# Most causal masks of two batches taken off the matrix engine, one batch's x transposed by DMA, and the order of work composed anew, in an attention and SwiGLU kernel

## The chip, the cores and the metric

The kernel runs on one core of a Trainium2 chip. The metric is the device time of a run in microseconds (us), which lies some 1.7 us above the span that the profile shows. Runs of this kernel vary: 0.9% among the first four of the kernel before, and more on the chip of the experiments. Each run has a state: here "slow" means over 1.5% above the fastest run of the same kernel. Ratios compare runs of the state "fast" alone. Each run also lists TensorE's mean granted clock, as a share of full speed.

## The reference

Attention with 16 beacon keys per head in front of 576 causal keys, then a SwiGLU block on the result. Shortened:

```python
B, H, S, Nb, D = 8, 8, 576, 16, 64
k_all = concat([beacon_k, k], axis=2); v_all = concat([beacon_v, v], axis=2)
scores = q @ k_all.T / sqrt(D)
scores = where(causal, -1e9, scores)       # beacons are visible to all
a = softmax(scores)
x = (a @ v_all) as [4608 tokens, 512]
out = (silu(x @ w_gate) * (x @ w_val)) @ w_out     # d_ff = 1536
```

## The kernel before

One core does it all in bf16 with fp32 accumulation. The order of work on every engine is fixed by a string, the *list*, of one letter per piece. The letters that matter here are `s` (a unit of scores with its exp), `P` (value products of one head), `X` (x of two heads transposed on TensorE), `g` and `G` (part of, or a full, gate and value unit), `F` (one output matmul), `l` (a load issued by GpSimd), `c`/`C` (a regrouping copy on VectorE/GpSimd), `t` (a DMA transpose of k or q). A unit of scores covers two heads and up to 496 columns; four of them (A to D) make a pair of heads.

A causal mask is needed only on the diagonal blocks. It is made in one of two ways. In batches 0 and 1 TensorE adds -30000 to the scores with a matmul before the exp; in batches 2 to 7 GpSimd zeroes the upper triangle of p with a select after it:

```python
PE_MASKS = (0, 1)
NPEX = 2                    # batches whose x is transposed on TensorE

def mask_on_pe(u, ps):
    for hh in range(2):
        for col, n, d in UNITS[u][3]:
            nc.tensor.matmul(ps[:, hh, col : col + n], lhsT=below[:],
                             rhs=ident[:, d : d + n], start=False, ...)

def exponent(b, m, u, ps):
    nc.scalar.activation(p[:, :, c0 : c0 + w], ps[:, :, 0:w], ACT.Exp, scale=0.125)
    for col, n, d in [] if b in PE_MASKS else diagonals:
        nc.gpsimd.affine_select(out=ap, in_=ap, ...)

def scores(burst):
    tiles = [big.tile([P, 2, 512], FP32, ...) for _ in burst]
    # ... the score matmuls of all units of the burst; exponent() at once,
    # or, for b in PE_MASKS, mask_on_pe() and exponent() after them all
# [cut]
        elif kind == "P":
            pv(b, m, n % 2, *small())
            if b >= NPEX and n % 8 == 7:
                x_transpose(b)          # five DMA transposes issued by SyncE
```

GpSimd also issues the loads that cast fp32 to bf16, which is all but the first three. In the list they begin with v of batch 0, then all eight gate and value weight loads, then k, q and v of batch 1:

```python
start = v_loads(0, 0, H)
for i in range(4):
    start += w_loads(i)
start += k_loads(1, 0, H) + q_loads(1, 0, H) + v_loads(1, 0, H)
```

A full gate and value unit is eight matmuls of 512 columns into a two-bank PSUM tile, a tanh on ScalarE and two passes of VectorE. Three such tiles (`big`) serve units of scores and gate units alike.

The softmax here doesn't subtract the row's maximum and nothing guards it: scores larger than these inputs give would overflow.

## Time and profile before

| | kernel before |
|---|---|
| time, median of the first 3 runs | 377.18 us (374.79 to 377.33) |
| profiled run, its span | 374.0 us, 372.3 us |
| TensorE busy | 364.0 us, 98% |
| matmuls | 2919 |
| mask matmuls on TensorE / selects on GpSimd | 80 / 120 |
| first full gate unit starts (timeline) | 28.81 us |

The prediction below shows the page's lines. A digit in the rows of slices is the busy share of one fortieth of the span in tenths. A wait is put down to what ended it. A timeline row gives start, length, engine, line, operation, shapes, count and, in brackets, the idle time before it and what ended that. The length uses a modelled end, so the cost of a matmul is better read from the difference of two starts.

### The profile page before, as it was taken

To read this page: it belongs to the slowest core of one execution; us is meant where nothing else is said; L and a number is where in the kernel's file an instruction comes from. 1 tells how busy PE (TensorE), PEld (TensorE's weight loads), DVE (VectorE), ACT (ScalarE), POOL (GpSimd) and SP (SyncE) were. 2 spreads that over 40 slices of the span, in tenths; PEclk is the share of its full clock that TensorE was granted. 3 is DMA by queue.
4 is the path that set the end of the run, shared out by engine and by line. 5 is a ranking of instruction groups with operands and counts; after the bars stand their busy time and mean duration, and the time that the engine had idled before them with its cause. 6 is when DMAs were issued, how large, how long until landed. Compare 5 with 4: busy or idle time off the path is not lost.

```text
span 372.3 us, 7423 instructions
## 1 busy us (share of the span) xinstructions
PE 364.0 (98%) x2919; PEld 184.2 (49%) x2919; DVE 230.9 (62%) x432; ACT 170.3 (46%) x243; POOL 154.4 (41%) x267
## 2 busy tenths in 40 slices
PE   8999999999999989999999999999999999999996
PEld 4654466554454544445455445544545444444443
DVE  5848845477646658555658476477565764666652
ACT  3943389833673644455562536723751311321210
POOL 8847789992893590453390602810320000000000
PEclk9999999999999999999999999999999999999999
DMA  9999999999999999794798792742100311001012
GB/s 168 178 203 160 180 158 162 148 185 95 124 205 145 72 117 172 90 101 78 129 149 91 123 148 72 78 51 60 58 28 30 63 58 56 0 30 57 30 40 102
DMA packets 158516, 39.04 MB, mean 105 GB/s; under 512 B 146576, under 2 KB 154000, under 8 KB 158480
## 3 DMA queue, kind: packets, MB, share of 16 engines
q0 software_dynamic: 112304, 18.83, 73.6%
q1 hardware_dynamic: 45968, 19.43, 24.4%
q8 instruction: 23, 0.38, 0.4%
q10 hardware_dynamic: 208, 0.29, 0.3%
q14 instruction: 13, 0.11, 0.1%
HBM read 38.27 MB, written 9.44 MB: 128 GB/s over the span
## 4 chain that ended last, share of the span: by engine, by line
PE 93%; DMA 3%; DVE 1%; POOL 1%; ACT 1%; issue 0%; POOLq 0%; ACTq 0%
PE gv_ps L355 49%; PE o_ps L394 24%; PE pv_ps L310 7%; PE s_ps L286 7%; DMA vb<-in_v_dram 2%; PE s_ps L255 2%; DMA first_k<-in_k_dram 1%; PE t_ps L234 1%; PE o_ps L414 1%; PE xt_ps L329 1%; PE t_ps L210 1%; POOL p L269 1%; ACT p L266 1%; POOL vb L138 0%; DVE kT L196 0%
## 5 line engine op out<-in xcount | busy, mean ns | idle before, releaser
L368 ACT ACTIVATE th<-gv_ps 128x512 f32<-128x512 f32 x108 | 64.4, 597 | 163.7 <-PE gv_ps L355 160.0
L370 DVE SCALAR_TENSOR_TENSOR u<-th,gv_ps 128x512 f32<-128x512 f32 x108 | 74.1, 686 | 76.5 <-ACT th L368 75.6
L355 PE MATMUL gv_ps<-xT,wg 128*128 128x512 bf16 x432 | 112.8, 379 | 1.5 <-DVE hT L373 1.3
L394 PE MATMUL o_ps<-wo,hT 128*128 128x512 bf16 x420 | 113.3, 380 | 0.0
L355 PE MATMUL gv_ps<-xT,wv 128*128 128x512 bf16 x432 | 112.8, 379 | 0.0
L266 ACT ACTIVATE p<-s_ps 128x992 bf16<-128x992 f32 (+2 forms) x128 | 101.9, 866 | 18.8 <-PE s_ps L286 14.6
L269 POOL TENSOR_SCALAR_AFFINE_SELECT p<-p 128x256 bf16<-128x256 bf16 (+2 forms) x120 | 44.3, 398 | 108.6 <-ACT p L266 108.4
L373 DVE SCALAR_TENSOR_TENSOR hT<-gv_ps,u 128x512 bf16<-128x512 f32 x108 | 74.6, 691 | 3.7
L355 PEld LDWEIGHTS <-wv 128*128 128x128 bf16 x432 | 42.2, 98 | 50.7
L355 PEld LDWEIGHTS <-wg 128*128 128x128 bf16 x432 | 41.3, 98 | 48.6 <-issue 2.2
L394 PEld LDWEIGHTS <-hT 128*128 128x128 bf16 x420 | 37.5, 98 | 41.9 <-issue 5.7
L310 PEld LDWEIGHTS <-p 128*128 128x128 bf16 x960 | 36.6, 97 | 11.2 <-DVE x L319 0.4
L310 PE MATMUL pv_ps<-vb,p 128*128 128x65 bf16 x960 | 39.6, 193 | 1.0 <-DMA vb<-in_v_dram 1.0
L138 POOL DMA_DIRECT2D vb<-in_v_dram x40 | 34.3, 870 | 0.7 <-PE pv_ps L310 0.3
L286 PE MATMUL s_ps<-qT,kT 64*128 64x80 bf16 (+4 forms) x384 | 33.7, 281 | 0.6 <-ACT p L266 0.3
L319 DVE TENSOR_TENSOR x<-pv_ps,rec 128x320 bf16<-128x320 f32 x64 | 31.4, 491 | 2.6 <-DVE rec L318 0.4
L138 POOL DMA_DIRECT2D kb<-in_k_dram x35 | 30.0, 858 | 6.7 <-DMA wv<-in_moe_w_val_dram 4.2
L403 DVE COPY o_sb<-o_ps 128x512 f32<-128x512 f32 x35 | 24.0, 685 | 13.9 <-PE o_ps L394 13.7
L138 POOL DMA_DIRECT2D qb<-in_q_dram x35 | 30.2, 864 | 5.3 <-PE t_ps L234 2.0
L318 DVE RECIPROCAL rec<-pv_ps 128x5 f32<-128x5 f32 x64 | 12.2, 190 | 31.1 <-PE pv_ps L310 31.0
L286 PEld LDWEIGHTS <-kT 64*128 64x128 bf16 x384 | 14.7, 94 | 19.6 <-issue 12.9
L255 PE MATMUL s_ps<-ident,below 128*128 128x128 bf16 (+1 forms) x80 | 7.9, 217 | 0.0
(52 smaller groups left out, 87.9 us busy)
## 6 DMA issues: line engine op xcount, KB each, us to landing
out_dram<-o_sb SPq DMA_DIRECT2D x35, 256.0 KB, 2.7
qb<-in_q_dram POOLq DMA_DIRECT2D x28, 128.0 KB, 5.7
vb<-in_v_dram POOLq DMA_DIRECT2D x24, 128.0 KB, 5.3
kb<-in_k_dram POOLq DMA_DIRECT2D x21, 128.0 KB, 7.0
wg<-in_moe_w_gate_dram POOLq DMA_DIRECT2D x4, 384.0 KB, 9.9
wv<-in_moe_w_val_dram POOLq DMA_DIRECT2D x4, 384.0 KB, 11.1
wo<-in_moe_w_out_dram POOLq DMA_DIRECT2D x2, 768.0 KB, 9.1
vb<-in_v_dram POOLq DMA_DIRECT2D x8, 112.0 KB, 5.1
```

Source lines behind the costliest of these rows:

```text
L138: return eng.dma_start(dst[p0 : p0 + n, c, h0:h1, 0:D], src[b, h0:h1, r : r + n, :].rearrange("h j d -> j h d"))
L266: nc.scalar.activation(p[:, :, c0 : c0 + w], ps[:, :, 0:w], ACT.Exp, scale=0.125)
L269: nc.gpsimd.affine_select(out=ap, in_=ap, compare_op=ALU.is_ge, fill=0.0, base=d, pattern=[[0, 2], [1, n]], channel_multiplier=-1,)
L286: nc.tensor.matmul(ps[:, hh, col : col + n], lhsT=kT[b % 2][r, m, P * t : P * t + P], rhs=qT[b % 2][r, m, q0 : q0 + n], start=b not in PE_ ...
L310: nc.tensor.matmul(o_ps[:, c, 0 : D + 1], lhsT=pt[(NPAIR * b + m) % NPT][:, hh, col : col + P], rhs=vb[b % 2][:, t, h, 0 : D + 1], start=( ...
L319: nc.vector.tensor_tensor(out=xs[b][:, :, D * h : D * h + D], in0=o_ps[:, :, 0:D], in1=rec[:].to_broadcast([P, NKT, D]), op=ALU.mult,)
L355: nc.tensor.matmul(gvs[f][:, TOK * half : TOK * half + TOK], lhsT=w[:, kk, P * f : P * f + P], rhs=xT[:, kk, r : r + TOK], start=(kk == 0) ...
L368: nc.scalar.activation(th[:], ps[:, 0:TOK], ACT.Tanh, scale=0.5)
L370: nc.vector.scalar_tensor_tensor(out=u[:], in0=th[:], scalar=1.0, in1=ps[:, 0:TOK], op0=ALU.add, op1=ALU.mult)
L373: nc.vector.scalar_tensor_tensor(out=hTs[j][:, f, :], in0=ps[:, TOK:1024], scalar=0.5, in1=u[:], op0=ALU.mult, op1=ALU.mult)
L394: nc.tensor.matmul(st["o"][:], lhsT=hTs[j][:, f, P * i : P * i + P], rhs=wo[:, f, :], start=(f == 0), stop=(f == NF - 1),)
L403: nc.vector.tensor_copy(o_sb[:], st["o"][:])
```

## The change

The intent is to unload TensorE, which is busy all the time: masks of the first two batches go mostly behind the exp, to VectorE (a multiply with a 0/1 triangle, new letter `d`) or GpSimd (the select, letter `e`); x of batch 1 goes to DMA transposes as in later batches; 36 masks of batches 2 to 7 go from GpSimd to VectorE; and the list is composed anew, with the weight loads as letters `w` in it.

```diff
-NPEX = 2
+NPEX = 1
-PE_MASKS = (0, 1)
+    upper = static.tile([P, P + NB], BF16, name="upper")
-    def exponent(b, m, u, ps):
+    def exponent(b, m, u, mask, ps):
-        for col, n, d in [] if b in PE_MASKS else diagonals:
+        for col, n, d in [] if mask == "s" else diagonals:
             ap = p[:, :, c0 + col : c0 + col + n]
+            if mask == "d":
+                nc.vector.tensor_tensor(
+                    out=ap, in0=ap, in1=upper[:, None, d : d + n].to_broadcast([P, 2, n]), op=ALU.mult
+                )
+                continue
             nc.gpsimd.affine_select(
@@ [cut: the same test in scores()] @@
-    start = v_loads(0, 0, H)
-    for i in range(4):
-        start += w_loads(i)
-    start += k_loads(1, 0, H) + q_loads(1, 0, H) + v_loads(1, 0, H)
+    weights = [load for i in range(4) for load in w_loads(i)]
+    start = v_loads(0, 0, H) + k_loads(1, 0, H) + q_loads(1, 0, H) + v_loads(1, 0, H)
@@ [cut: 17 early parts of gate units become 9; all 20 lines of the list; the first two:] @@
-        "llllllclqlllKcllKssclQlcccslsllKlsQssKQsllllsPlP",
-        "ssPlsPXslossXPsllPgPlXollgPglgXlggglgllgGGlGlGGl",
+        "lllllllclQkcKeeQcdscwCwKeslcQssQKsswPwPeePPewXee",
+        "XPllsPgPxgllPwggXlllgwlgwogggGGllGGGGoGlGulGFddF",
```

More of the change, by code (lines that the diff above doesn't have):

```diff
@@ L177, in load_wo @@
         )
-    spare = []
     def parts_of(eng):
@@ L200, in transpose_pair @@
         h = slice(2 * m, 2 * m + 2)
-        while spare:
-            spare.pop()
-            nc.tensor.transpose(t_ps[:, 0:P], below[:], ident[:])
         first = n - 64
@@ L281, in scores @@
         tiles = [big.tile([P, 2, 512], FP32, name="s_ps", tag="big") for _ in burst]
-        for (b, m, u), ps in zip(burst, tiles):
+        for (b, m, u, mask), ps in zip(burst, tiles):
             for t, col, q0, n in UNITS[u][2]:
@@ L289, in scores @@
                         rhs=qT[b % 2][r, m, q0 : q0 + n],
-                        start=b not in PE_MASKS or col == 0,
-                        stop=b not in PE_MASKS,
-                    )
-            if b not in PE_MASKS:
-                exponent(b, m, u, ps)
-        for (b, m, u), ps in zip(burst, tiles):
-            if b in PE_MASKS:
+                        start=mask != "s" or col == 0,
+                        stop=mask != "s",
+                    )
+            if mask != "s":
+                exponent(b, m, u, mask, ps)
+        for (b, m, u, mask), ps in zip(burst, tiles):
+            if mask == "s":
                 mask_on_pe(u, ps)
-                exponent(b, m, u, ps)
+                exponent(b, m, u, mask, ps)
     xs = {}
@@ L453 @@
     )
+    nc.gpsimd.memset(upper[:], 1.0)
+    nc.gpsimd.affine_select(
+        out=upper[:],
+        in_=upper[:],
+        compare_op=ALU.is_ge,
+        fill=0.0,
+        base=0,
+        pattern=[[1, P + NB]],
+        channel_multiplier=-1,
+    )
     idle = big.tile([P, 1024], FP32, name="idle_ps", tag="big")
@@ L485 @@
     done = dict.fromkeys("SPKQUXgGFltwoc", 0)
-    first = ([(0, 0, 2), (1, 0, 2), (0, 2, 3), (1, 2, 3), (2, 0, 2), (2, 2, 3), (0, 3, 4), (1, 3, 4), (2, 3, 4)],
-             [(0, 0, 1), (0, 1, 2), (1, 0, 1), (1, 1, 2), (0, 2, 3), (1, 2, 3), (0, 3, 4), (1, 3, 4)])
-    parts = [(j, *part) for j in range(2) for part in first[j]]
-    units = [(j, f) for j in range(NCH) for f in range((3, 2, 0)[min(j, 2)], NF)]
+    first = [[(0, 0, 2), (1, 0, 2), (0, 2, 3), (1, 2, 3), (2, 0, 2), (2, 2, 3), (0, 3, 4), (1, 3, 4), (2, 3, 4)]]
+    parts = [(j, *part) for j in range(len(first)) for part in first[j]]
+    units = [(j, f) for j in range(NCH) for f in range((3, 0)[min(j, 1)], NF)]
     def free(b, values=False):
@@ L520, in piece @@
     def piece(kind):
-        n = done[{"C": "c", "k": "K", "q": "Q", "u": "U", "x": "X", "Y": "K", "Z": "Q", "s": "S"}.get(kind[0], kind[0])]
+        n = done[{"C": "c", "k": "K", "q": "Q", "u": "U", "x": "X", "Y": "K", "Z": "Q", "s": "S", "d": "S", "e": "S"}.get(kind[0], kind[0])]
         eng = nc.scalar if kind in "kqx" else nc.gpsimd if kind == "C" else None if kind in "YZ" else nc.vector
-        if kind[0] == "s":
+        if kind[0] in "sde":
             burst = []
@@ L531, in piece @@
                     assert done["U"] > i // 4 - 4 if b < NPE else done["t"] >= 10 * (b - NPE + 1)
-                burst.append((b, m, ("ABDC" if b == 0 else "ABCD")[i % 4]))
+                burst.append((b, m, ("ABDC" if b == 0 else "ABCD")[i % 4], kind[i - n]))
             scores(burst)
@@ L554, in piece @@
             assert done["X"] >= 4 * j + k1
+            assert done["w"] >= 2 * (f // 3) + 2
             gv_mm(j, f, k0, k1)
@@ L560, in piece @@
             assert j < NHT or done["F"] >= (j - NHT + 1) * 4 * NF
-            assert done["g"] >= (9, 17)[j] if j < 2 else done["P"] >= 8 * min(j + 1, B)
+            assert done["g"] >= 9 if j < 1 else done["P"] >= 8 * min(j + 1, B)
+            assert done["w"] >= 2 * (f // 3) + 2
             gv_unit(j, f)
@@ L570, in piece @@
         elif kind == "w":
-            spare.extend(range(4))
+            weights[n]()
         elif kind in "cC":
@@ L581, in piece @@
             turns[n]()
-        done[{"C": "c", "k": "K", "q": "Q", "u": "U", "x": "X", "Y": "K", "Z": "Q", "s": "S"}.get(kind[0], kind[0])] += len(kind)
+        done[{"C": "c", "k": "K", "q": "Q", "u": "U", "x": "X", "Y": "K", "Z": "Q", "s": "S", "d": "S", "e": "S"}.get(kind[0], kind[0])] += len(kind)
     one_bank = [(outp, "outp")]
@@ L586 @@
     plan = [
-        "llllllclqlllKcllKssclQlcccslsllKlsQssKQsllllsPlP",
-        "ssPlsPXslossXPsllPgPlXollgPglgXlggglgllgGGlGlGGl",
-        "GlGUGGsFFlFFusUlslFFssFFlssFFlFFPulssFllPssFPlll",
-        "FsslFllPssFPUsFtxUssXllFtlFUttstPlFFssslFlFPUsFF",
-        "FPsssFFFlPFtlFssglgPsllltlsFFFXtFggXgllgPFgFgtGP",
-        "GltGPFllGlGlFGFGFsstFFPFFtllstssFltPttlFGPllGlGF",
-        "FssFllFFFFsslsPFFFFFPstlssFFtFFFltPslsFFFFlPFFtF",
-        "lGGlGlFGFGFFssFPFFlFFFlsssFPFGPllFtGFFssPFtltFll",
@@ L595 @@
-        "lFFlsstsltPFFGPGFGlFGFGGGFFFstsFtFFFFltFFFFlssll",
-        "GGtFGPGFslsFFlFlFPtssstFFFtPltFFFGFFGFGFFPFFFFFF",
-        "FsslsPFFFFFlFPFstssFlFFGFFPGGFFFssttFFlFFlFlsssl",
-        "FFFFPGlFFPltsltsFFlFFslssFPFGPFGFFGFtPGtGttFFFFP",
-        "FGFFtltssFFFFFlPssslFFFFttFFlFGtFtFGGFGGFFGGlGFl",
-        "FFPFFFtsssFFFFtPFFsssPFFFFFFPssslFFllFPFFFsssPFF",
-        "FFFFFFFlFsssFPlFGFGFGGFFPFGFGFlFGFGGFFFGssFPFFFG",
-        "FFssFFFPFFFsssPFFGGFGFssFFFPFFFFFsssPFFFFFFFFFFF",
-        "PFGPFFGFFFPFFFGFFGFGGFGGFFFFFFFGFFFFFGFFFFFFFFFF",
@@ L604 @@
-        "FFFGFFFFFFFGFFFFFFGFGFFGGGFFFGFFFGFFGFFFFGFFFGFF",
-        "FGFFGFFFFFFFFFFFFFGFFFFFFFFFFFFGFGFGGGFFFGFFFFFF",
-        "FFFFFFFFFFFFFFFFFFFFFFFFFFFFFFFFFFFFFFFFFFFFFFF",
+        "lllllllclQkcKeeQcdscwCwKeslcQssQKsswPwPeePPewXee",
+        "XPllsPgPxgllPwggXlllgwlgwogggGGllGGGGoGlGulGFddF",
+        "lllFFFFUddlllllFlFlFllFlFFUdeFFFPUlddlPFFdeeFFFF",
+        "PFllFlFdePeeFFlPuFFlllPdeeFFPueFPFdeFlFFtFUeeFFF",
+        "PFlFdeelPFtUePtFFeeFPFdeelFPFlllGllGGPtGtGlllGlG",
+        "lllPGlGGGllGllllFlFFltttttedFPlFFteetFFFFtFFeeel",
@@ new lines @@
+        "PFtllFFFFFtPddeFtFPFFltFFledePllFFFFFFdddFllFltF",
+        "FltPGGPlGtFllGtlPFGtGGGtGGlPttGllFddFllFFFFFlFdt",
+        "eeFFFtFlGFddFPtlFFFFdeeFtFFtFlFFPdleeFFFFlFFFlFP",
+        "FFeleldPFFGlGttFtFGFGlFFFFPFFFllldeeFPFtGFFeePFF",
+        "FdeetFFFPFlGlGGFtGGlFtPFGGlGFlFllFFFFFPFtFldeePF",
+        "FFGPGFFFlFlFlFteeFFFFeteelFPFGlteldFFFFPFFGFFFFG",
+        "tFlFGGFFFFFFFPFeeleFFFFPGGtGGFFFteeFFFPlFFtFleed",
+        "tFFFGGPGFGtGPlGFFtFFdeFFFFFPFFeeetlPFFtGGGFFFFFF",
+        "FFFFPeddFFFFPFFlFdedFFFFFPGGGFFFFFFlFeeFFFFFPeee",
@@ L607 @@
+        "FFFFFFPFFFFFFPeedFFFFFFFFFFPdeeFFPGFFFGPGGFGFPFG",
+        "GPFFGFGFGFFGGFFFFFFFFFFFFFGFFFFGFFFFGFGFFFFFFFFF",
+        "FFFFFGGFFFFGGGGFFFFGGFFFFFFFFFFFFFGFFGFFFFFGFFFG",
+        "FFFFFFFGFFFFFFFGFGFFFFFGFGGFFGFGFFFFFFFFFFFFFFFF",
+        "FFFFFFFFFFFFFFFFFFFFFFFFFFFFFFFFFFFFF",
     ]
-    for kind in re.findall("sss(?!s(?!s))|ss?|.", "".join(plan).replace("S", "ss")):
+    for kind in re.findall("[sde]{3}(?![sde](?![sde]))|[sde]{1,2}|.", "".join(plan)):
         piece(kind)
-    del done["w"]
@@ L611 @@
-    assert done == dict(S=16 * B, P=8 * B, K=4, Q=4, U=4 * (NPE - 1), X=4 * NPEX, g=17, G=len(units), F=4 * NF * NCH, o=2, c=6, l=len(loads), t=len(turns)), done
+    assert done == dict(S=16 * B, P=8 * B, K=4, Q=4, U=4 * (NPE - 1), X=4 * NPEX, g=9, G=len(units), F=4 * NF * NCH, w=8, o=2, c=6, l=len(loads), t=len(turns)), done
 _INS = ['q', 'k', 'v', 'beacon_k', 'beacon_v', 'moe_w_gate', 'moe_w_val', 'moe_w_out']
```

## The prediction

> **What bounds the kernel now.** I read the page's busy table and slices first, then the chain of waits, then TensorE's waits, then its timeline, and the busy time by stretch last. The table, the slices and the chain:
>
> ```profile
> PE 364.0 (98%) x2919; PEld 184.2 (49%) x2919; DVE 230.9 (62%) x432; ACT 170.3 (46%) x243; POOL 154.4 (41%) x267
> PE   8999999999999989999999999999999999999996
> ACT  3943389833673644455562536723751311321210
> DMA  9999999999999999794798792742100311001012
> ...
> PE 93%; DMA 3%; DVE 1%; POOL 1%; ACT 1%; issue 0%; POOLq 0%; ACTq 0%
> ```
>
> TensorE is busy for 98% of the 372.3 us span and carries 93% of the chain that ended last. The DMA row is full in the first 16 slices (150 us) and ScalarE's in slices 2, 6 and 7 (9.3 to 18.6 us and 46.5 to 65.1 us); either could take over if TensorE's load falls there. TensorE's list of waits, all of it after the start:
>
> ```profile
> PE gv_ps L355 <- DVE hT L373: 1.3, 1, 1.3
> PE idle_ps L458 <- DVE p L434: 1.3, 1, 1.3
> PE pv_ps L310 <- DMA vb<-in_v_dram: 1.0, 1, 1.0
> PE s_ps L286 <- ACT p L266: 0.3, 1, 0.3
> ```
>
> So after the start some 3 us of visible waiting can be won; the rest is work. Busy time uses modelled ends (a 512-column matmul counts 379 ns), so I priced TensorE's work by start-to-start times in its timeline:
>
> ```profile
> 28.81 1.02 PE L355 MATMUL gv_ps<-xT,wg 128*128 128x512 bf16 x4 [1.27 <-DVE hT L373]
> ...
> 29.67 1.03 PE L355 MATMUL gv_ps<-xT,wv 128*128 128x512 bf16 x4
> ...
> 55.36 0.47 PE L255 MATMUL s_ps<-ident,below 128*128 128x128 bf16 x6
> 55.67 0.38 PE L394 MATMUL o_ps<-wo,hT 128*128 128x512 bf16 x1
> ```
>
> Four gate matmuls take 29.67 - 28.81 = 0.86 us, 216 ns each. Six mask matmuls take 55.67 - 55.36 = 0.31 us, 52 ns each; over all groups of masks 50 to 60 ns. Five x transposes take 0.26 to 0.28 us in the same view, 54 ns each. The start is different; ScalarE's timeline has
>
> ```profile
> 8.74 9.43 ACT L266 ACTIVATE p<-s_ps 128x992 bf16<-128x992 f32 x12 [1.53 <-PE s_ps L255]
> 18.40 3.13 ACT L266 ACTIVATE p<-s_ps 128x992 bf16<-128x992 f32 x4 [0.22 <-PE s_ps L255]
> ```
>
> Those are all 16 exps of batch 0, from 8.74 to 21.53 us with one gap of 0.22 us: (9.43 + 3.13) / 16 = 0.79 us each. Until 21.5 us ScalarE sets the pace, although TensorE looks busy.
>
> **What the Trainium skill says.** "TensorE: Matmul & The Clock Gate", section "Wait — 56ns, not 53.3ns?", gives start-to-start N / 2.4 GHz + 2.5 ns when warm: 55.6 ns at 128 columns, 215.7 at 512. The trace agrees (50 to 60, and 216), so a mask matmul costs its columns, not its 217 ns of busy time. "VectorE: DVE Perf Modes", section "The perf-mode tier table", has tensor_tensor on bf16 in SBUF at two elements a cycle and 1224 ns for 2048 elements; scaled with the fixed 150 cycles of the section before it, 256 elements are (128 + 150) / 0.96 = 290 ns, an estimate; nothing in this trace shows it, the kernel has no such operation yet. "SBUF — State Buffer", section "SBUF: two separate sides", says that a VectorE operation with two SBUF inputs and a GpSimd operation that reads SBUF exclude each other for a whole instruction. The new multiplies are of that kind; no run here shows it yet. "VectorE: DVE Perf Modes", section "The three transpose paths", has 1309 ns for a 128x128 DMA transpose; here its issue takes 1.19 to 1.37 us for 128x512 and it lands after 3.5 us (median), so in the trace as well it is slow but off the engines.
>
> **The change, part by part.**
> 1. *Masks.* The lists of instructions show 80 mask matmuls on TensorE before and 20 after, and all 20 in batch 0. So batch 1 loses 40 x 0.055 = 2.2 us of TensorE work and batch 0 loses 20 x 0.055 = 1.1 us. Batch 1's is on the path. Batch 0's is mostly not, as ScalarE sets the pace there; what can be won is the first exp's start: the mask matmuls at 8.44 stand between its scores and it. The first exps may begin up to 0.4 us earlier. I count 0.3 us.
> 2. *Their replacements.* VectorE gets 49 multiplies x 0.29 = 14 us: from 230.9 to some 245 us, 66% of the span. 36 of these come from GpSimd's batches 2 to 7. GpSimd's selects go from 120 to 101, at 0.35 to 0.40 us (44.3 us for 120): 7 us less. In total neither is near its limit. A mask now stands between exp and the value product, as in batches 2 to 7 before, where TensorE never waited for one in the list above. No time, as long as the list leaves that distance.
> 3. *x of batch 1.* 20 of 40 x transposes leave TensorE: 20 x 0.054 = 1.1 us, on the path. With them go four copies out of PSUM (7 to 3 on VectorE, 0.46 us each; they weren't bounding). SyncE gets five transposes, 5 x 1.3 = 6.6 us of its queue plus about 4 us to land: 11 us from the last value product of batch 1 to x in place. In the new list, priced with the step costs above, 53.8 - 64.6 = 10.8 us of TensorE work lie between these and the first gate matmul of tokens 512 to 1023, which needs four of the five. Just hidden.
> 4. *The list with weight loads in it.* The bytes are the same. Weights 5 to 8 now come behind batch 1's k and most of q (about 1.0 MB in bf16). Loads run at about 0.18 MB/us in this stretch (the page's 160 to 200 GB/s): the last weight lands 5 to 6 us later, near 37 us instead of 31. The unit that first needs it is the seventh full one, 10.4 us after the first; before, the first started at 28.81, so it is needed near 39. Hidden by about 2 us. The second half of the output weights comes as before (about 46 us, wanted near 48).
> 5. *Waits.* The 1.27 us for hT at 28.8 us comes of three units in the three PSUM tiles whose last quarters are done together; the new list has the same nine parts in the same order, so it stays. The 1.03 us for vb at 133 us comes of a load stuck behind masks in GpSimd's list; the new list spreads these, so I count 0.8 us won.
>
> Sum: -2.2 - 1.1 - 0.3 - 0.8 = -4.4 us; against it 0.9 us for new small waits (below). Net -3.5 us, or -0.9%.
>
> **Rivals.**
> - *ScalarE becomes the bound in batch 1.* Before:
>
> ```profile
> 50.00:60.00 10.00, 10.00 (x167) 7.19 (x167) 4.03 (x12) 9.49 (x14) 9.51 (x14) 1.00 2.31 170
> 60.00:70.00 10.00, 10.00 (x150) 6.45 (x148) 6.57 (x17) 9.17 (x13) 9.79 (x16) 1.00 1.96 137
> ```
>
> (the columns are the stretch, its length, then busy time of PE, PEld, DVE, ACT, POOL). ScalarE was at 9.49 and 9.17 of 10 us. The new list has the 32 units of batches 1 and 2 in 28.3 us of TensorE work; ScalarE needs 32 x 0.79 + three PSUM copies x 0.65 = 27.2 us for it. That is 96%: any jitter becomes a TensorE wait. For it: the numbers. Against it: three score tiles of slack and the old list's 93% with hardly any wait. Price if it holds: up to 2 us, and the gain shrinks to 1.5 us.
> - *GpSimd's list blocks.* Its masks now stand among DMA issues of 0.8 us each, and those wait for earlier transfers (waits of 1 to 2 us at 19 to 31 us before). A mask of batch 0 behind a blocked issue delays value products, x and the first gate unit. I place the last batch-0 select near 21.3 us, just ahead of its exp's end; the first blocked issue before came at 19 us. Price: 0 to 2 us at the start.
> - *A late transfer* (x of batch 1, or a weight): 0 to 3 us, by the thin margins above. The DMA row is full there. Against it: landing times in the loaded stretch were 7.0 us at most.
> - *More than the sum:* if the new list gets VectorE to release PSUM sooner at the start, the 1.27 us goes and first gate units come earlier by the whole 1.1 us of batch 0: -6 us. Only with that and a favourable draw is 2% (7.5 us) reached.
>
> **Range and chances.** 377.18 - 3.5 = 373.7; but the three runs before lie at 374.79 to 377.33 with the median at the upper end, and the profiled one at 374.0, so another draw is more likely lower than higher, which I put at -0.7: 373.0 us. The spread of 2.5 us among runs and the 0 to -6 us (with +2 for the transfers) of the rivals give 369.3 to 377.2 as the range. Faster by over 2% means below 369.6: 0.09. Slower by over 2% needs two rivals at their worst and more: 0.03. The rest is 0.88.
>
> **What would show it.** Right: TensorE's busy share still 97 to 98%; the chain again some 93% TensorE with the mask share (1.6%) cut to 0.4%; 2919 - 80 = 2839 matmuls; new multiplies of 0.25 to 0.35 us; first exp at 8.3 to 8.5 us; first full gate unit still near 28.5 us after a wait of 1.3 us for hT; span 367 to 370 us. Wrong: a TensorE wait of over 1 us for ScalarE's exps between 45 and 75 us, for an x transpose or a gate weight between 35 and 80 us, or for a mask before 22 us; a mask multiply of 0.5 us or more, held up by GpSimd; or a first gate unit that moved by more than 1.5 us either way.

## The result

| | before | changed |
|---|---|---|
| median of 4 runs | 377.25 us (374.79 to 378.04) | 372.6 us (371.73 to 373.42) |
| ratio of the fast runs | | 0.9885 (95%: 0.984 to 0.993) |
| profiled run: span, mean clock | 372.3 us, 0.999 | 371.5 us, 0.986 |
| matmuls | 2919 | 2839 |
| mask matmuls / multiplies / selects | 80 / 0 / 120 | 20 / 49 / 101 |

A ratio is the mean time of one kernel's fast runs over that of the other's of the same rounds, so it isn't quite the ratio of the medians. The changed kernel takes 1.1% less time; the 2% test calls it "same".

The changed kernel's page, the same rows as before and the clock's:

```profile
PE 363.1 (98%) x2839; PEld 181.9 (49%) x2839; DVE 241.6 (65%) x474; ACT 171.5 (46%) x245; POOL 149.9 (40%) x251
PE   7998999999989999999999999999999999999996
ACT  4753369963466348554255444544642311311210
PEclk9599999999999999999999999999999999999999
DMA  9999999999999999999959279036200301001003
...
PE 75%; DMA 13%; POOL 8%; issue 2%; ACT 1%; DVE 0%; POOLq 0%
```

TensorE is as busy as before. Three things differ. The clock row has a 5 in slice 2. The DMA row stays full to slice 20 (186 us) instead of 16. And the chain that ended last now runs through DMA and GpSimd for 21% of the span instead of 4%.

TensorE's list of waits in the changed kernel, to be set against the four lines in the prediction:

```profile
PE pv_ps L309 <- DMA vb<-in_v_dram: 1.6, 3, 0.7
PE gv_ps L354 <- DVE hT L372: 1.3, 1, 1.3
PE idle_ps L467 <- DVE p L433: 1.3, 1, 1.3
PE t_ps L201 <- DVE qT L193: 0.4, 1, 0.4
PE s_ps L285 <- ACT p L260: 0.3, 1, 0.3
```

The list is as short as before, but the wait for v grew from 1.0 to 1.6 us. The start is where the picture changes. ScalarE's exps of batch 0 in the changed kernel (before they were two rows, with one gap of 0.22 us):

```profile
8.24 3.14 ACT L260 ACTIVATE p<-s_ps 128x992 bf16<-128x992 f32 x4 [0.51 <-PE s_ps L285]
11.64 1.83 ACT L260 ACTIVATE p<-s_ps 128x992 bf16<-128x992 f32 x2 [0.25 <-PE s_ps L285]
13.85 1.41 ACT L260 ACTIVATE p<-s_ps 128x416 bf16<-128x416 f32 x2 [0.38 <-PE s_ps L249]
16.77 1.83 ACT L260 ACTIVATE p<-s_ps 128x992 bf16<-128x992 f32 x2 [1.51 <-PE s_ps L249]
18.93 1.41 ACT L260 ACTIVATE p<-s_ps 128x416 bf16<-128x416 f32 x2 [0.33 <-PE s_ps L285]
20.84 3.29 ACT L260 ACTIVATE p<-s_ps 128x992 bf16<-128x992 f32 x4 [0.50 <-POOL p L268]
```

The first exp comes at 8.24 instead of 8.74 us, but now there are five gaps, 2.97 us in all, and the last exp ends at 24.1 instead of 21.5 us. TensorE's timeline has the first full gate unit accordingly late:

```profile
31.49 1.02 PE L354 MATMUL gv_ps<-xT,wg 128*128 128x512 bf16 x4 [1.27 <-DVE hT L372]
```

31.49 - 28.81 = 2.68 us later than before. In this stretch TensorE's clock was down. The two stretches from 10 to 20 us (stretch, length, then busy time and count of PE, PEld, DVE, ACT, POOL, then clock, DMA share, GB/s), before:

```profile
10.00:20.00 10.00, 10.00 (x184) 7.25 (x180) 7.57 (x20) 9.64 (x13) 7.78 (x11) 1.00 1.63 183
```

and changed:

```profile
10.00:20.00 10.00, 9.90 (x118) 6.87 (x117) 6.02 (x13) 7.53 (x11) 8.63 (x14) 0.52 1.52 128
```

After the first full gate unit it is the other way round. From there to the end of the last matmul the kernel before took 368.86 - 28.81 = 340.05 us, the changed one 368.38 - 31.49 = 336.89 us, so 3.2 us less. (A second profile of the changed kernel gave 336.06 us.) Part of what was won there was lost again at one place, where TensorE waits for v of batch 3, load by load:

```profile
104.95 0.28 PE L309 MATMUL pv_ps<-vb,p 128*128 128x65 bf16 x4 [0.56 <-DMA vb<-in_v_dram]
105.90 0.31 PE L309 MATMUL pv_ps<-vb,p 128*128 128x65 bf16 x5 [0.67 <-DMA vb<-in_v_dram]
106.54 0.19 PE L309 MATMUL pv_ps<-vb,p 128*128 128x65 bf16 x1 [0.32 <-DMA vb<-in_v_dram]
```

These 15 small matmuls began at 104.06 us and the next piece at 106.57 us: 2.5 us, where 0.45 is usual in the same timeline.

The profile of before was one of its quick runs (374.0 us against a median of 377.25), so the two spans show a smaller gain (372.3 to 371.5 us) than the times do. I therefore judge by the runs' times and use the profiles to find places.

### The profile page after: what moved, and what is told of

Its sections match the earlier page's. It is cut to its first block, busy times and chain, and to the rows that moved or that the text cites. A ratio compares the mean times of both kernels' runs of the same rounds, so it can differ in the third digit from the quotient of the medians.

```text
span 371.5 us, 7274 instructions
## 1 busy us (share of the span) xinstructions
PE 363.1 (98%) x2839; PEld 181.9 (49%) x2839; DVE 241.6 (65%) x474; ACT 171.5 (46%) x245; POOL 149.9 (40%) x251
## 4 chain that ended last, share of the span: by engine, by line
PE 75%; DMA 13%; POOL 8%; issue 2%; ACT 1%; DVE 0%; POOLq 0%
PE gv_ps L354 39%; PE o_ps L393 23%; DMA kb<-in_k_dram 6%; PE pv_ps L309 6%; PE s_ps L285 5%; DMA vb<-in_v_dram 5%; DMA wg<-in_moe_w_gate_dram 2%; POOL qb L137 2%; POOL vb L137 2%; POOL kb L137 1%; POOL p L268 1%; ACT p L260 1%; PE o_ps L413 1%; PE t_ps L228 1%; POOL wg L166 0%
## 5 line engine op out<-in xcount | busy, mean ns | idle before, releaser
L393 PE MATMUL o_ps<-wo,hT 128*128 128x512 bf16 x420 | 109.8, 380 | 0.0
L268 POOL TENSOR_SCALAR_AFFINE_SELECT p<-p 128x256 bf16<-128x256 bf16 (+2 forms) x101 | 37.5, 393 | 98.9 <-ACT p L260 92.9
L309 PE MATMUL pv_ps<-vb,p 128*128 128x65 bf16 x960 | 40.6, 195 | 1.6 <-DMA vb<-in_v_dram 1.6
L264 DVE TENSOR_TENSOR p<-p,upper 128x256 bf16<-128x256 bf16 (+2 forms) x49 | 13.4, 289 | 22.8 <-ACT p L260 22.5
```

What stands on the lines that cost most here:

```text
L268: nc.gpsimd.affine_select(out=ap, in_=ap, compare_op=ALU.is_ge, fill=0.0, base=d, pattern=[[0, 2], [1, n]], channel_multiplier=-1,)
L309: nc.tensor.matmul(o_ps[:, c, 0 : D + 1], lhsT=pt[(NPAIR * b + m) % NPT][:, hh, col : col + P], rhs=vb[b % 2][:, t, h, 0 : D + 1], start=( ...
L393: nc.tensor.matmul(st["o"][:], lhsT=hTs[j][:, f, P * i : P * i + P], rhs=wo[:, f, :], start=(f == 0), stop=(f == NF - 1),)
```

## The experiments

All ran on one chip, in three calls. In those calls the kernel before ran 101 times, 16 of them in the slow state: medians of all 376.09, 376.08 and 375.48 us (of the fast ones 375.39, 375.22 and 374.79), with single runs from 372.28 to 381.26 us. The changed kernel itself ran in the first call only. In some of the traces a few matmul records are missing (2792 of 2839 in the second profile of the changed kernel), so I use starts and waits from them, not busy sums.

### First call: where batch 0 loses its time

**The changed kernel again.**

> The changed kernel itself, so that the others of this call are compared with it on one chip. Both theories: ratio to before 0.985 to 0.992; in the profile TensorE's clock falls to about half between 10 and 20 us (0.52 in that stretch in the first profile) and the first full gate unit starts at 31.5 us instead of 28.8. If the low clock was an accident of that one run, this profile shows 0.95 or more between 10 and 20 us and the first full gate unit near 28.5 us.

Measured: 371.71 us (6 runs), ratio 0.9896 (0.9848 to 0.9944). The clock again fell to half, this time from about 15 to 19 us (0.83 over 10 to 20 us); the first full gate unit started at 30.92 us. This trace, with the clock still full at 14 us, shows where the delay starts. TensorE, GpSimd (three rows) and ScalarE in the timeline:

```profile
14.83 0.43 PE L204 MATMUL t_ps<-ident,kb 96*128 96x96 bf16 x6 [1.33 <-POOL kb L193]
...
12.38 0.84 POOL L268 TENSOR_SCALAR_AFFINE_SELECT p<-p 128x224 bf16<-128x224 bf16 x2
13.17 0.77 POOL L166 DMA_DIRECT2D wg<-in_moe_w_gate_dram  x1
13.94 0.84 POOL L193 COPY kb<-ks 96x768 bf16<-96x768 bf16 x1
...
16.19 1.83 ACT L260 ACTIVATE p<-s_ps 128x992 bf16<-128x992 f32 x2 [1.77 <-PE s_ps L249]
```

The copy that regroups k for a later pair of heads was given to GpSimd. There it stands behind loads, two selects of batch 0 and a weight load. TensorE waits 1.33 us for it, and ScalarE then has nothing to exponentiate for 1.77 us. Here the wait comes before the fall of the clock. In the first profile it was the other way round: the clock fell at 9.27 us, and the slowed TensorE did not have to wait for the copy. One more thing delays GpSimd's list: the triangle for the multiplies is made there (0.48 and 0.37 us, from 5.2 us on), so its loads of v begin at 6.06 instead of 5.19 us. No run moved that.

**All masks of batch 0 back on TensorE.**

```diff
-        "lllllllclQkcKeeQcdscwCwKeslcQssQKsswPwPeePPewXee",
+        "lllllllclQkcKssQcsscwCwKsslcQssQKsswPwPssPPswXss",
```

> All masks of batch 0 back on TensorE (10 units, 20 matmuls more), the rest as in the changed kernel. Theory C (the 20 mask matmuls taken out of batch 0 kept TensorE busy enough for its full clock): the clock stays at 0.95 or more between 10 and 20 us, the first full gate unit starts at 28.3 to 29.3 us, the span is 1.5 to 2.7 us under the changed kernel's although TensorE does 1.1 us more. Theory G (the late start comes of masks behind blocked DMA issues in GpSimd's list, the clock being only a by-product): also near 28.8 us, so this run alone does not tell C from G; the filler run does.

Measured: full clock in its profile, first full gate unit at 29.45 us, span 368.6 us; but 372.15 us over 18 runs, ratio 0.9913 (0.9881 to 0.9945). The expected 1.5 us shows in the profile and not in the times. Six of the 18 runs had a mean clock below 0.9985, and those had spans of 371.1 to 373.2 us against a mean of 369.65 us for the other twelve.

**Filler matmuls.**

```diff
+            if b == 0 and mask != "s":
+                for hh in range(2):
+                    for _ in UNITS[u][3]:
+                        nc.tensor.matmul(ps[:, hh, 0:P], lhsT=below[:], rhs=ident[:], start=True, stop=True)
```

> The changed kernel with 20 matmuls of 128 columns ahead of batch 0's scores, whose results are overwritten: TensorE has the mask matmuls' load back, the masks stay where the change put them. Theory C (clock): clock 0.95 or more between 10 and 20 us, first full gate unit at 28.3 to 29.5 us, span 1.5 to 2.7 us under the changed kernel's. Theory G (masks on GpSimd late): the clock may recover, but the first full gate unit stays at 31 us or later and the span does not fall.

Measured: clock 1.00 throughout 10 to 20 us in its profile, first full gate unit at 30.35 us; 372.38 us (13 runs), ratio 0.9907 (0.9874 to 0.9940). TensorE still waits 0.8 us for GpSimd's copy. The unit starts 0.6 to 1.1 us earlier than in the two profiles of the changed kernel (31.49 and 30.92 us), and 30.35 - 28.81 = 1.5 us of the delay stay. This doesn't yet divide the delay: the 20 matmuls take some 1.1 us themselves (20 x 0.055), and four later traces have this batch 0 at full clock without them (see "The clock and the spread of runs"). The times show no gain, and in 5 of the 13 runs the mean clock was below 0.9985 despite the filler.

**v of batch 3 loaded before k and q of batch 4.**

```diff
-        loads += (kq_then(b + 1) if b + 1 < B else []) + v_then(b)
+        kq = kq_then(b + 1) if b + 1 < B else []
+        loads += v_then(b) + kq if b == 3 else kq + v_then(b)
```

> The changed kernel with the v loads of batch 3 issued before the k and q loads of batch 4 instead of after them. If the 2.1 us that TensorE loses at 104 to 107 us waiting for v of batch 3 is only a matter of the loads' order: that wait goes, no other of over 0.5 us appears, span down by 1.5 to 2.1 us. If DMA is simply short there: a wait for k or q of batch 4 (or their transposes) takes its place and the span moves by under 0.7 us.

Measured: the wait for v is gone from the list; 371.18 us (6 runs), ratio 0.9879 (0.9828 to 0.9931). That is 0.5 us under the changed kernel in the same call, well within the intervals. In its place the profile has waits of 0.4 us each for k of batch 2 and for the output weights, and one of 1.0 us for a copy of q at 5.2 us, ahead of anything that this edit touches. The earlier load removes the wait in this profile; but the k copy run below has no such wait either, with the old order of loads, so the order isn't shown to be its cause. What mending it gains is too small to be told here.

### Second call: the parts one by one

**Only batch 1's masks moved, in the old kernel with the old list, to GpSimd.**

```diff
-PE_MASKS = (0, 1)
+PE_MASKS = (0,)
```

> The kernel before with its old list; only the 40 mask matmuls of batch 1 are replaced, by GpSimd selects behind the exp (as batches 2 to 7 have them). If TensorE's removed work is on the path as predicted: 40 x 0.055 = 2.2 us less, ratio to before 0.993 to 0.996. If GpSimd's list, at 95 to 100% busy between 50 and 80 us in the kernel before, holds the selects up: value products of batch 1 wait for masks, ratio 0.998 or more.

Measured: 380.52 us (6 runs), ratio 1.0188 (1.0124 to 1.0251): slower than before, though the 2% test calls it "unclear". TensorE's largest wait, and the stretch in which it falls (columns as above):

```profile
PE pv_ps L310 <- POOL p L269: 3.9, 5, 1.0
...
55.00:60.00 5.00, 4.25 (x44) 2.77 (x44) 1.77 (x5) 2.12 (x4) 5.00 (x12) 0.50 1.40 133
```

GpSimd is busy for all 5.00 us: selects alternate with load issues of 0.7 to 0.9 us. TensorE's clock is at half from 54.4 to 61.2 us. Removing 2.2 us of matmuls this way costs some 7 us by the ratio.

**x of batch 1 on TensorE again, soon after its value products.**

```diff
-NPEX = 1
+NPEX = 2      # and four X in the list, each two pieces behind its P
```

> The changed kernel with x of batch 1 transposed on TensorE again (20 transposes, four copies out of PSUM), two list steps behind its value products; the rest unchanged. Predicted part: 1.1 us more TensorE work, so 1.1 us slower than the changed kernel. Rival D (the DMA transposes of batch 1's x delay the loads behind them, and this is what makes TensorE wait for v of batch 3 at 104 us): that wait shrinks from 1 to 2 us to under 0.5 us, and the run is as fast as the changed kernel or faster.

Measured: 374.53 us (14 runs), ratio 0.9964 (0.9935 to 0.9993). TensorE waited 2.3 us for VectorE to write x, which is a fault of where I put the letters. So this run mixes two things; its repeat is below.

**The k copy on VectorE.**

```diff
-        "lllllllclQkcKeeQcdscwCwKeslcQssQKsswPwPeePPewXee",
+        "lllllllclQkcKeeQcdscwcwKeslcQssQKsswPwPeePPewXee",
```

> The changed kernel with one letter of the list changed: the regrouping copy of k of heads 2 and 3 or 4 and 5 in batch 0 that the list gives to GpSimd goes to VectorE. Theory G (GpSimd's list holds up batch 0: this copy stands behind six v loads, two k loads, two selects and a weight load, and TensorE waits 1.3 us for it): the wait for the copy goes, the gap of 1.8 us in ScalarE's exps at 14.4 us shrinks below 0.6 us, the first full gate unit starts 1.0 to 1.8 us earlier than 30.9 us, and the kernel gets 1.0 to 1.8 us faster. If the selects, not the copy, are what holds batch 0 up: the gap moves to a later exp and the gain is under 0.5 us.

(The copy is in fact the one for heads 6 and 7.) Measured: the wait for the copy is gone, the first full gate unit starts at 29.74 us, which is no earlier than in traces that have the copy on GpSimd and the clock full (29.63 to 30.22 us, see below); 370.91 us (12 runs), ratio 0.9914 (0.9883 to 0.9945). The expected gain of 1.0 to 1.8 us is not established: 0.8 us by the medians of two calls, none by the ratios. The profile shows what took its place, in TensorE's list of waits:

```profile
PE gv_ps L354 <- DMA wv<-in_moe_w_val_dram: 1.5, 1, 1.5
```

TensorE now reaches its first gate part at 20.2 us, before the first value weights are there. In the changed kernel that wait was hidden behind the delay. From the first full gate unit to the end this run took 338.41 us (368.15 - 29.74), 2.3 us more than the second profile of the changed kernel; its list has new waits of 0.8 us for k of batch 2 and 0.4 us for x. The profiled run was the slowest of the twelve (372.95 us).

**All three together** (k copy on VectorE, batch 0's masks on TensorE, v of batch 3 earlier; the diffs above).

> Everything that the first runs point to in one kernel: the changed kernel with that copy on VectorE, batch 0's masks all on TensorE, and v of batch 3 loaded ahead of k and q of batch 4. If the parts add (late batch 0: 2 us, wait for v: 1 us): 2 to 3 us faster than the changed kernel, ratio to before 0.981 to 0.985. If the lost time comes back at the next full engine: under 1 us.

Measured: 371.18 us (6 runs), ratio 0.9898 (0.9852 to 0.9944), against an expected 0.981 to 0.985. In the profile the first full gate unit is at 29.08 us; new waits of 0.9 us for a select and 0.6 us for q appear later. The parts do not add.

### Third call: the parts undone in the changed kernel

**x of batch 1 on TensorE, better placed** (each X some eight pieces behind its P).

> As the run with x of batch 1 on TensorE, but each transpose of x stands some eight list steps behind the value product that it needs instead of two: in that run TensorE waited 2.3 us for VectorE to write x (1.8 us at one place), so its 0.7% loss mixes the work with a placement fault. Predicted part: 1.1 us slower than the changed kernel (ratio about 0.992 to 0.995 against 0.990). Rival D (the DMA transposes cost as much in late loads as they save): no wait for v of batch 3 over 0.4 us and ratio within 0.002 of the changed kernel's.

Measured: 374.22 us (22 runs), ratio 0.9975 (0.9953 to 0.9997): 0.8% or 2.5 us (medians) above the changed kernel, where 1.1 us was predicted. The changed kernel's six runs are of another call, and with both intervals the 0.8% may be 0.3 to 1.3% (1 to 5 us): more than predicted is likely, how much more isn't shown. The wait for v of batch 3 is gone, as rival D had it (and as in the k copy run, where x stays on DMA), but another came, at 62 to 69 us:

```profile
PE pv_ps L309 <- DVE xT L193: 1.4, 2, 1.0
```

x comes out of PSUM through the one tile that value products also use at this point. A value product has to wait until VectorE has copied x out. The DMA route frees TensorE from 1.1 us of work *and* this tile from four copies.

**Batch 1's masks on TensorE.**

```diff
-        ... "oGlGulGFddF", "lllFFFFUdd...UdeFFFPUlddlPFFdeeF", "...FdePeeF...PdeeFFP..."
+        ... "oGlGulGFssF", "lllFFFFUss...UssFFFPUlsslPFFsssF", "...FssPssF...PseeFFP..."
```

> The changed kernel with batch 1's masks (16 units) on TensorE again, 40 matmuls; its list, batch 0 and x of batch 1 stay as changed. Predicted part: 2.2 us slower than the changed kernel (ratio 0.995 to 0.997). If the selects and multiplies cost as much as they save: within 0.7 us of it.

Measured: 375.13 us (22 runs), ratio 1.0009 (0.9983 to 1.0035): 1.1% or 3.4 us (medians) above the changed kernel, where 2.2 us was predicted (2.2 to 6.3 us with both intervals, so the excess is likely rather than shown). The work itself is 2.2 us; a rest of about that size is visible as a wait that the changed kernel does not have:

```profile
PE pv_ps L309 <- ACT p L260: 1.3, 1, 1.3
```

In a burst of units the masks are matmuls after all scores, so by the order in the code the exp starts later, and the value product meets it at 67 us.

**All masks of batches 1 to 7 on GpSimd** (every `d` in the list from batch 1 on becomes `e`).

> The changed kernel with the 48 masks of batches 1 to 7 that VectorE multiplies given to GpSimd (12 of batch 1, 36 later). Theory V (it is VectorE's share that keeps masks from standing behind DMA issues in GpSimd's list; with the old list and GpSimd alone TensorE waited 3.9 us for selects, its clock fell to half for 8 us and the kernel was 1.9% slower than before): waits for selects of 1 us or more between 50 and 70 us, 2 to 7 us slower than the changed kernel. If the recomposed list alone does it: no such wait and within 1 us of the changed kernel.

Measured: 382.7 us (6 runs), ratio 1.0202 (1.0158 to 1.0246; "unclear" by the 2% test against the kernel before): 3.1% slower than the changed kernel. TensorE's largest wait and its worst place in the timeline:

```profile
PE pv_ps L309 <- POOL p L268: 5.7, 4, 4.0
...
61.19 0.62 PE L309 MATMUL pv_ps<-vb,p 128*128 128x65 bf16 x5 [3.96 <-POOL p L268]
```

GpSimd issues ten loads of k and q in a row there, from 52.34 to 60.7 us, and the selects stand behind them. The clock fell to 0.66 over 60 to 70 us. The longest wait for a select in the changed kernel is below the 0.2 us that the list shows.

**The k copy on VectorE and the first two weight loads ahead of the first k loads.**

```diff
-        "lllllllclQkcKeeQcdscwCwKeslc...
+        "llllllwwcQkcKeeQcdsclclKeslc...
```

> The changed kernel with the k copy on VectorE and the first two weight loads ahead of batch 1's first two k loads and of the selects in GpSimd's list (two letters swapped with two others). In the run with the copy alone the wait for the copy went and TensorE waited 1.5 us for the first value weights instead. If GpSimd's order of loads is all that is left there: no wait for weights, first full gate unit at 28.0 to 28.6 us instead of 29.7, 1.0 to 1.5 us faster than the run with the copy alone, ratio 0.980 to 0.988. If another wait takes its place: under 0.5 us.

Measured: 372.01 us (11 runs), ratio 0.9903 (0.9872 to 0.9934). Its profile fell in the slow state with a low clock at the start and at 100 to 120 us, so it is not compared. Over the runs there is no gain: inconclusive on the mechanism, and not a better kernel.

None of these versions is clearly faster than the changed kernel.

### The clock and the spread of runs

Every run lists its mean clock. Over the fast runs of the kernel before on this chip: 55 with a clock of 0.9985 or more have a mean span of 372.8 us, 30 with a lower one 374.8 us. Over the ten runs of the changed kernel (both chips' calls): three with full clock 370.2 us, seven with a lower one 370.5 us. So the changed kernel gains 2.6 us on runs at full clock and 4.3 us on the others. Its own clock falls in batch 0 in both of its profiles. The kernel before was traced once, at full clock; where its clock falls in its slower runs is not known, and with ten runs this difference is an observation, not a proof.

The kept traces say more about batch 0. In four runs the edit comes later in the list and batch 0 is the changed kernel's as it is: x of batch 1 on TensorE (both), batch 1's masks on TensorE, all masks on GpSimd. All four have the full clock in batch 0 without any filler, although TensorE waits 1.0 to 1.2 us for the k copy. The one with x better placed, stretch and first full gate unit:

```profile
10.00:20.00 10.00, 8.19 (x145) 5.66 (x142) 7.49 (x19) 8.54 (x13) 9.29 (x16) 1.00 1.53 133
...
29.85 1.02 PE L354 MATMUL gv_ps<-xT,wg 128*128 128x512 bf16 x4 [1.27 <-DVE hT L372]
```

The four start their first full gate unit at 29.63, 29.85, 29.89 and 30.22 us, so at full clock the changed batch 0 is 0.8 to 1.4 us late, and the low clock goes with another 0.7 to 1.9 us in the two profiles of the changed kernel. It need not cost that: with v of batch 3 loaded earlier the clock was at half from 7.6 to 14.5 us, and the unit started at 29.75 us.

So the full clock in the runs with filler or with masks on TensorE doesn't show that the added matmuls kept it up. In all 14 traces the clock changes only at whole multiples of about 3.41 us after its first rise (5.86, then 9.27 and 19.51 us in the first profile; 5.33, then 15.57 and 18.98 us in the second), and this first rise lies anywhere from 4.07 to 7.27 us. The four traces whose clock fell in batch 0 had it at 4.07 to 5.86 us; of the other ten, which kept it there, nine had it at 6.19 us or later and one at 5.15 us. Where this grid happens to lie may thus matter as much as the edit; no run tests it.

## Why the prediction was right, and where its steps were not

The predicted 373.0 us met 372.6 us, and its net 0.9% met 1.1%. The total is right partly because wrong terms cancelled.

- *Bound.* Right: TensorE stayed 98% busy, with 2839 matmuls. But the prediction expected the chain to stay at 93% TensorE; it fell to 75% (85% in the second profile), with DMA and GpSimd in most of the rest. The span, forecast at 367 to 370 us, was 371.5 and 370.1 us. Two readings were off: ScalarE's row has an 8, not a 9, in slice 6, and landing times "of 7.0 us at most" are the page's median for k; its gate and value weights took 9.9 and 11.1 us.
- *Masks of batch 1, "2.2 us on the path".* The mechanism is right, the size probably too small: undone in the changed kernel it costs 3.4 us by the medians. The term counted the matmuls and left out that they stand between scores and exp (the wait of 1.3 us).
- *"No time, as long as the list leaves that distance".* Right for the changed list and VectorE's share, and only for these: with the old list and GpSimd alone the same move cost 1.9%, with the new list and GpSimd alone 3.1% against the changed kernel. The prediction treated the 14 us of multiplies as a load on VectorE to be paid for; they are what makes the change work.
- *Multiplies, "0.25 to 0.35 us".* Right: 49, median 0.291 us, 13.4 us in all (0.234 to 0.466 us over three shapes).
- *x of batch 1, "1.1 us".* Probably too small: 2.5 us by the medians, for the PSUM tile that the prediction dismissed with "they weren't bounding". "Just hidden" is right: TensorE doesn't wait for batch 1's x in the profiles of the changed kernel (in the k copy run it waits 0.4 us for x).
- *Batch 0, "0.3 us".* This step failed. The first exp did come early (8.24 us, within 8.3 to 8.5 but for 0.06), but the first full gate unit came 2.1 to 2.7 us late instead of at 28.5 us, beyond the 1.5 us that the prediction named as a sign of being wrong. Some 0.8 to 1.4 us of it are there at full clock too and go with the second rival, priced at 0 to 2 us and counted within the 0.9 us for small waits. It came through a k copy moved to GpSimd, which the prediction had overlooked among the letters. The rest goes with the low clock, which was in no rival.
- *Waits, "0.8 us won" on v.* This step failed too: the wait went from one place (1.0 us at 133 us) to another (1.6 us at 104 to 107 us). The DMA row also stays full for longer. The DMA transposes of x add to the queue, but they aren't the reason: with x of batch 1 back on TensorE, two steps behind its value products, the row is full to slice 20 as well. The DMA queue of transposes and stores, before:

```profile
q1 hardware_dynamic: 45968, 19.43, 24.4%
```

and changed (packets, MB, share of 16 engines' span):

```profile
q1 hardware_dynamic: 48432, 20.02, 28.8%
```

  With x of batch 1 back on TensorE the wait is gone, and with an earlier issue of v too; but so it is in the k copy run, which changes neither. Its cause stays open, and none of these runs is faster than the changed kernel by more than the noise.
- *Weights.* Right as far as it went: no wait for them in the changed kernel. The k copy run shows the margin at the *first* weights, not at the last ones that the prediction worked out.
- *ScalarE as the bound in batch 1.* Didn't come: its longest hold on TensorE is 0.3 us.

Left open: why the clock falls in batch 0 in some executions and not in others, and how the rest of the delay divides between the k copy, the selects and the triangle made on GpSimd. The single repairs of batch 0 bring the first full gate unit forward by 0.6 to 2.4 us only when they are set against the two profiles with a low clock. Against the four traces at full clock (29.63 to 30.22 us) all three together are 0.6 to 1.1 us earlier and masks on TensorE 0.2 to 0.8 us; the k copy alone shows nothing clear, and the filler run is later. That these repairs hardly show in the times fits this. Later waits for transfers and selects, different in each run, may take the remainder; no run separates them.

## What to carry to other kernels

GpSimd both computes and issues DMAs here, and its selects came after the load issues ahead of them in its list: before giving such an engine work, read what stands ahead of that work in its list, not its busy share, and keep work that the critical engine awaits out of it. When an operation leaves the critical engine, count also the chain that it stood in and the buffer that it held; here that added, by the medians, 1.2 and 1.4 us to savings of 2.2 and 1.1 us. Compare two profiles only where their clocks agree: what looked like 1.2 us won by the k copy (30.92 to 29.74 us) is no gain beside profiles at full clock. On a kernel this full, a repair at one place is worth its time only if the next transfer or queue is ready earlier too, so check it by the times of many runs and not by the place in the profile.

## What the Trainium skill lacked or had wrong

- "TensorE: Matmul & The Clock Gate", section "HAM oscillation — how this bites in real kernels", puts the fall of the clock down to idle gaps of more than about 3.4 us; its next section adds frequent micro-idles. In this case the clock was at half from 9.27 to 19.51 us with no wait of TensorE over 0.4 us in the 4 us ahead of it (3.22 of them busy); the page gives no measure of how much short idling is enough. In another run it halved at 54.4 us after waits of 0.2, 1.0 and 0.8 us, 2.0 us in all in the 2.5 us ahead.
- "GPSIMD Engine Reference", section "4.1 Engine selection", advises on speed per operation. That GpSimd's queue is strictly in order stands elsewhere ("PSUM — Partial Sum Buffer", section "Engine vs sequencer instructions"). This section lacks what follows from it and decided here: a compute operation waits behind DMA issues, each 0.7 to 0.9 us, ten in a row for 8.3 us, and TensorE waited 3.96 us for a 0.4 us select.
- "VectorE: DVE Perf Modes", section "The perf-mode tier table": the estimate of 290 ns scaled from it for a 256-element bf16 multiply agrees with the measured median of 291 ns over all shapes (307 ns is the mean of the 31 with 256 elements); nothing to mend.
- "SBUF — State Buffer", section "SBUF: two separate sides", on VectorE and GpSimd excluding each other: 46 of the 49 multiplies took 0.234 to 0.294 us over three shapes; the other three took 0.447 to 0.466 us, two of them while a GpSimd select ran. No run here separates a hold-up by GpSimd from other causes.
